# A Sinkhorn gate without GpSimd, eleven products at the attention's end, and earlier left-over tiles in the last layer

## The chip, the core and the metric

The kernel runs on one core of a Trainium2 chip. TensorE multiplies matrices into PSUM (eight banks of 128 partitions x 512 fp32 columns), VectorE (DVE), ScalarE (ACT) and GpSimd (POOL) do the element work, and SyncE (SP) issues nearly all transfers. The metric is the device time of one execution in microseconds, as the median of several runs. Lines such as L410 are lines of the kernel before.

## What is computed

Three layers follow one another. The inputs are drawn once with a fixed seed.

```python
# attention with random features: B, H, S, D = 4, 8, 576, 64; 128 features
h = proj(x) - sum(x * x) / 2;  phi = exp(h - max(h)) / sqrt(128)
out = (phi(q) @ (phi(k).T @ v)) / (phi(q) @ sum(phi(k)) + 1e-6)
# -> x of 2304 tokens x 512

# mixture of 8 experts with a balanced gate
P = np.exp(logits - logits.max())            # logits = x @ w_gate, 2304 x 8
for _ in range(8):
    P /= P.sum(1, keepdims=True) + 1e-09
    P /= P.sum(0, keepdims=True) + 1e-09
    P *= N / E
for e in range(E):
    out += P[:, e:e+1] * (np.maximum(x @ w1[e], 0.0) @ w2[e])      # 512 -> 1024 -> 512

# last layer: 512 -> 768 -> 512
h = np.maximum(np.maximum(x @ w1, x @ w2), x @ w3)
out = h @ w_out
```

## The kernel before

**Products.** Every fp32 matrix is split into a high and a low part, and the first multiplication of each layer is done by a scheme of Strassen's kind: seven products instead of eight, of sums and differences of operands. `sub_products` writes such a set. It works for half the width of the experts' middle layer at a time, so `s` counts sub-experts: s = 0 and 1 are the two halves of expert 0. One product is six matmuls of 128x384 (L410 to L412) into one of three banks, `ub`, `vb`, `wb`. Two of the three keys alternate between sets (`bu0`/`bu1`, `bv0`/`bv1`), `bw` is the same in all. ScalarE copies what is needed twice (`u1`, `u5`, `u2`, L417), VectorE adds it to a bank (`plus`, L217), and the sum is a result: (0,0) and (1,1) leave from `wb`, (0,1) from `vb`, (1,0) from `ub`. `relu_results` makes each result into a pair of high and low operands `h` (ScalarE L456, VectorE L457). A bank has 512 columns, of which a product uses Q = 384.

**Tiles.** `tile_out` is the second multiplication: six matmuls of 128x512 (L480 to L482) into one of three banks in turn (`next_r`: `r0`, `r1`, `r2`), added by VectorE to the accumulator `acc` (L495, later with the gate's weight, L502 and L503). The six tiles of one set wait in a queue, and `take()` writes one of them between two products of the next set.

**Order.** `program()` generates the products, tiles and all vector work as tasks with costs. TensorE's order is the order of the code. For the other engines and for the transfers a planner (`Tasks.ordered`) simulates the costs and chooses the order; some tasks may go to VectorE or to GpSimd. Waits between engines are derived from the tiles that instructions use, for PSUM by whole banks.

**The attention's end.** The attention runs in 16 steps of two heads, each a chain over several engines. Behind each of its last code points TensorE gets one product of the expert layer (`feed_forward()`, `next(layers)`), at most FILL = 9; then the logits of the gate (L1227, L1235), their transposes (L1245) and the rest of s = 0 and 1 follow. In these first two sets there are only three banks, so `bu0`, `bv0` and `bw` serve both.

**The gate.** `gate()` is a generator with eleven pieces; from the fourth product of s = 1 on, a piece is written before 2 of 5 products. First the maximum of all logits is found: per partition by VectorE (L655), across partitions by GpSimd (`partition_all_reduce`, L656), negated (L657), and ScalarE takes the exponential (L658). Each of eight rounds then has five VectorE operations for the rows (sum, + 1e-9, reciprocal, multiply, sums of columns: L661 to L665, with `rs` and `cs` in SBUF), a matmul with a matrix of ones that sums the columns over the partitions (L670, into one of `r0` to `r2`), and four VectorE operations (L671 to L674). The weighted tiles of the next expert need the result.

**The last layer.** It has three phases (ph 3 to 5), each of three groups n of three sets m, 7 products each; q = 7m + i counts a group's products. A group's six tiles are left over for the next group: in the first group of phase 3 one is written after each product, everywhere else after q = 3, 6, 9, ... (L951). The first sets of phases 4 and 5 read operands `x` that `load_x` brings back from memory.

Of the kernel before, what the change touches and what calls it, by code (L numbers as in the profile page):

```python
# [21 lines left out]
ORDER_1 = [(0, 0), (3, 3), (4, 4), (1, 1), (5, 5), (6, 2), (2, 6)]  # L22
ORDER_2 = [0, 2, 3, 5, 4, 1, 6]

FILL = 9
SLACK = 6000
START = [("load", 0), ("squared", 0), ("squared", 1), ("norms", 0, 0), ("v", 1), ("load", 1), ("v", 0)]

# [126 lines left out]
def tile_performer__moe__max3(ctx, tc, kq_t, kq, v1, omega2, w_gate, w1, w2, m1, m2, m3, m_out, out):  # L155
    nc = tc.nc
# [28 lines left out]
    ident = const.tile([P, P], F32, name="ident")  # L185
    prob = const.tile([P, NT, E], F32, name="prob")
    mx = const.tile([P, 2], F32, name="mx")
    rs = const.tile([P, NT, 1], F32, name="rs")
    cs = const.tile([P, 1, E], F32, name="cs")
    pt = const.tile([2 * N // 3 // P * E, P], F32, name="pt")  # L190

# [64 lines left out]
    def t_(k):  # L256
        return ts[k]
# [126 lines left out]

    u_turn = [0, 0, 1]
    r_turn = [0]

    def next_r():  # L390
# [3 lines left out]
    def sub_products(k, before, results, xs=None):  # L394


        xs = xs or x_home
        n = u_turn.pop(0)
        u_turn.append(1 - u_turn[-1])
        ub, vb, wb = f"bu{n}", f"bv{n}", "bw"  # L400

        def product(i, j, b, onto):
            before(i, j)
            kh, kl = w_keys(k, i)

            def run():
                ps, w, x = banks[b][:, :Q], ws[k][:, i].rearrange("p c (k f) -> p c k f", k=2), [xs(j, c)[0]() for c in range(2)]
                given = dict(skip_group_check=onto)
                for c in range(2):
                    nc.tensor.matmul(ps, w[:, 0, c], x[c][:, 0], start=c == 0 and not onto, stop=False, **given)  # L410
                    nc.tensor.matmul(ps, w[:, 0, c], x[c][:, 1], start=False, stop=False, **given)  # L411
# [12 lines left out]
        yield  # L424
        to_u("u1", ub)
        product(*p[1], vb, False)
        yield
        to_u("u5", vb)
        product(*p[2], ub, True)
        yield  # L430
        to_u("u2", ub)
        product(*p[3], wb, False)
        yield
        results(0, 0, wb, lambda b, plus=plus: plus(wb, wb, "u1"), ("u1", wb))
        product(*p[4], ub, True)
        yield
        results(1, 1, wb, lambda b, plus=plus: plus(wb, ub, "u5"), ("u5", ub))
        product(*p[5], vb, True)
        yield
        results(0, 1, vb, lambda b, plus=plus: plus(vb, vb, "u2"), ("u2", vb))  # L440
        product(*p[6], ub, True)
        yield
        results(1, 0, ub, None, (None, ub))
# [204 lines left out]
    def gate():  # L648
        flat = prob.rearrange("p t e -> p (t e)")

        def dve(run, r, w):
            add("D", 250, lambda e: run(), r, w)

        dve(lambda: nc.vector.memset(t_("ones"), 1.0), [], ["ones"])
        dve(lambda: nc.vector.tensor_reduce(out=mx[:, 0:1], in_=flat, axis=AX.X, op=ALU.max), ["prob", "ones"], ["mx0"])  # L655
        add("P", 3000, lambda e: nc.gpsimd.partition_all_reduce(mx[:, 1:2], mx[:, 0:1], P, bass.bass_isa.ReduceOp.max), ["mx0"], ["mx1"])  # L656
        dve(lambda: nc.vector.tensor_scalar_mul(mx[:, 1:2], mx[:, 1:2], -1.0), [], ["mx1"])  # L657
        add("A", 300, lambda e: nc.scalar.activation(flat, flat, AF.Exp, bias=mx[:, 1:2]), ["mx1"], ["prob"])  # L658
        yield
        for _ in range(8):  # L660
            dve(lambda: nc.vector.tensor_reduce(out=rs, in_=prob, axis=AX.X, op=ALU.add), ["prob"], ["rs"])  # L661
            dve(lambda: nc.vector.tensor_scalar_add(rs, rs, 1e-9), [], ["rs"])
            dve(lambda: nc.vector.reciprocal(rs, rs), [], ["rs"])
            dve(lambda: nc.vector.tensor_tensor(out=prob, in0=prob, in1=rs.to_broadcast([P, NT, E]), op=ALU.mult), ["rs"], ["prob"])
            dve(lambda: nc.vector.tensor_reduce(  # L665
                out=cs[:, 0, :], in_=prob.rearrange("p t e -> p e t"), axis=AX.X, op=ALU.add
            ), ["prob"], ["cs"])
            yield
            b = next_r()
            pe(150, lambda b=b: nc.tensor.matmul(banks[b][:, :E], t_("ones"), cs[:, 0, :], start=True, stop=True), ["ones", "cs"], [b])  # L670
            dve(lambda b=b: nc.vector.tensor_scalar_add(cs[:, 0, :], banks[b][:, :E], 1e-9), [b], ["cs"])  # L671
            dve(lambda: nc.vector.reciprocal(cs, cs), [], ["cs"])
            dve(lambda: nc.vector.tensor_scalar_mul(cs, cs, float(N) / E), [], ["cs"])
            dve(lambda: nc.vector.tensor_tensor(out=prob, in0=prob, in1=cs.to_broadcast([P, NT, E]), op=ALU.mult), ["cs"], ["prob"])  # L674
        yield
        b = next_r()
        late = prob[:, PT:, :].rearrange("p t e -> p (t e)")
        pe(110, lambda: nc.tensor.transpose(banks[b][: 2 * PT * E, :P], late, ident), ["prob"], [b])
        act(P, lambda: nc.scalar.copy(pt, banks[b][: 2 * PT * E, :P]), [b], ["pt"])
        dma(48, lambda: prob_t.rearrange("t e c -> (t e) c"), lambda: pt, ["pt"], ["prob_t"])  # L680
        yield
# [3 lines left out]
    def program():  # L685
# [19 lines left out]
        for s in range(SUBS):  # L705
            if s:
                prepare_w1(s)
            else:
                w1_store(0)
            if s == SUB_E + 1:  # L710
                for _ in gating:
                    pass
            e = s // SUB_E
            for i, _ in enumerate(sub_products(s % 2, no_loads, relu_results(s % 2))):
                if i >= (1 if s > 1 else 3):
                    take()
                if s == 1 and i == 3:
                    gating = gate()
                if gating:
                    if gate_wait[0] % 5 in (0, 2):  # L720
                        next(gating, None)
                    gate_wait[0] += 1
            while queue:
                take()
            rest = prepare_w2(s, s == 0)
            if e == 0:
                evict = evict_raw(s == 0)
            else:
# [201 lines left out]
        for ph in (3, 4, 5):  # L930
            back = ph == 4
            xs = x_beside if back else x_home
            for n in range(3):
# [3 lines left out]
                for m in range(3):  # L937
                    a = 3 * n + m
                    slot = (a + 1) % 2
                    mat = 8 - a if back else a  # L940

                    def before(i, j, a=a, slot=slot, mat=mat):
                        kh, kl = w_keys(slot, i)
                        if ph == 3 or a > 1:
                            dma(256, lambda: ws[slot][:, i].bitcast(F32), lambda: lc1[mat][i], [("lc1", mat)], kh + kl)
                        if a == 0:
                            load_x(ph, j, xs)

# [348 lines left out]
    with tc.manual_schedule():  # L1297
# [4 lines left out]
        with left as att:  # L1302
# [7 lines left out]
            ts.update({f"w2_{k}": a.tile([P, 1024], F32R, name=f"w2_{k}") for k in range(2)})  # L1310
            ts.update({f"h{k}": a.tile([P, 2, Q], F32R, name=f"h{k}") for k in range(14)})
            banks.update({k: new_bank("po") for k in ("bu0", "bv0", "bw")})
            ring["b"] = "ph"
            layers = feed_forward()
            n = 0
            for _ in steps:
                if n < FILL:
                    next(layers)
                    n += 1
        while n < FILL:  # L1320
            next(layers)
            n += 1
        banks.update({k: new_bank("ph") for k in ("bu1", "bv1", "r0", "r1")})
        banks["r2"] = new_bank("small")
        b = ctx.enter_context(tc.tile_pool(name="b", bufs=1, side="left", reuse_waits="tile"))
        ts.update({f"w2_{k}": b.tile([P, 1024], F32R, name=f"w2_{k}") for k in range(2, 7)})
        ts.update({k: b.tile([P, Q], F32, name=k) for k in ("b11", "b12", "b21", "b22", "t1", "t2", "t3", "t4")})
# [61 lines left out]
```

## Time and profile before

| | |
|---|---|
| median of three runs | 1910.83 us (1908.7 to 1912.18) |
| the profiled execution | 1908.9 us; its span 1907.1 us |
| TensorE (PE) busy | 1864.3 us, 98% of the span |
| share of the last chain on PE | 89% |
| VectorE / ScalarE / GpSimd busy | 76% / 48% / 55% |
| mean granted clock | 0.993 |

A busy share is an average over stages. Rows of the timeline have the start in us, the duration in us, engine, line, operation, output and inputs, and in brackets the idle time of the engine before it with what released it. Matmuls overlap, so the pitch from start to start counts, not the duration: 0.175 us for a 128x384 and 0.23 us for a 128x512 at the full clock.

### The profile page before, as it was taken

The page shows a single profiled execution, that of the slowest core. Times are in us where ns is not written, and L with a number is a line of the kernel's source. Part 1 is how long each engine was busy: PE and PEld are TensorE (multiplying, and loading weights), DVE is VectorE, ACT ScalarE, POOL GpSimd, SP SyncE. Part 2 cuts the span into 40 slices and gives each one's busy share as a digit, 9 for nine tenths or more (in the row PEclk, how much of TensorE's full clock was granted, in tenths as well). Part 3 has the DMA queues.
Part 4 walks back from the last instruction along what each step waited for, and adds up shares of the span by engine and source line. Part 5 has one row for each costly group of instructions (what it writes and reads, how often), then busy time and mean ns, then how long its engine had stood idle before and what let it go on. Part 6 is the DMA issues. An engine that isn't in the chain of part 4 may idle for free.

```text
span 1907.1 us, 34485 instructions
## 1 busy us (share of the span) xinstructions
PE 1864.3 (98%) x11521; PEld 1769.9 (93%) x11521; DVE 1456.7 (76%) x2639; ACT 915.9 (48%) x2180; POOL 1045.2 (55%) x970
## 2 busy tenths in 40 slices
PE   8996899999999999999999999999999999999998
PEld 6885799999999999999999999999999999989998
DVE  7875998888888767888888888988888776443445
ACT  7874355555544465454454445544544543232221
POOL 4533777676545247576766786767776754320000
PEclk9998999999999999999999999999999999999999
DMA  7655699988877999998999899999999999997573
GB/s 238 198 178 198 229 313 324 330 298 319 270 248 248 316 307 337 327 286 286 332 306 305 269 347 300 309 304 286 302 321 312 323 352 355 342 336 252 209 242 117
DMA packets 376033, 547.06 MB, mean 287 GB/s; under 512 B 31568, under 2 KB 226992, under 8 KB 375856
## 3 DMA queue, kind: packets, MB, share of 16 engines
q1 hardware_dynamic: 375856, 544.86, 84.8%
q8 instruction: 91, 1.49, 0.3%
q14 instruction: 86, 0.70, 0.1%
HBM read 392.65 MB, written 152.09 MB: 286 GB/s over the span
## 4 chain that ended last, share of the span: by engine, by line
PE 89%; DVE 4%; DMA 4%; issue 1%; ACT 1%; POOL 1%; SPq 0%; DVEq 0%; ACTq 0%; POOLq 0%
PE po L410 9%; PE po L411 8%; PE po L412 8%; PE ph L410 6%; PE ph L412 6%; PE ph L411 6%; PE ph L822 5%; PE ph L820 5%; PE ph L821 5%; PE ph L480 4%; PE ph L482 4%; PE ph L481 4%; PE small L822 3%; PE small L820 3%; PE small L821 3%; PE small L482 2%
## 5 line engine op out<-in xcount | busy, mean ns | idle before, releaser
L217 POOL TENSOR_TENSOR h<-b,h 128x384 fp32r<-128x384 f32 x149 | 163.6, 1106 | 125.5 <-ACT h L760 124.4
L410 PE MATMUL po<-x,wa 128*128 128x384 f32 x676 | 227.4, 336 | 5.1 <-DVE po L217 2.3
L411 PE MATMUL po<-x,wa 128*128 128x384 f32 x676 | 226.9, 336 | 0.0
L412 PE MATMUL po<-x,wa 128*128 128x384 f32 x676 | 226.8, 336 | 0.0
L217 POOL TENSOR_TENSOR g<-g,g 128x256 f32<-128x256 f32 (+2 forms) x164 | 163.1, 996 | 86.2 <-DVE g L217 32.4
L412 PE MATMUL ph<-x,wa 128*128 128x384 f32 x588 | 198.6, 338 | 9.3 <-DVE wa L217 9.3
L822 PE MATMUL ph<-h,w 128*128 128x384 f32 x598 | 202.3, 338 | 0.0
L820 PE MATMUL ph<-h,w 128*128 128x384 f32 x598 | 202.0, 338 | 0.0
L821 PE MATMUL ph<-h,w 128*128 128x384 f32 x598 | 201.4, 337 | 0.0
L217 DVE TENSOR_TENSOR po<-po,u 128x384 f32<-128x384 f32 x230 | 129.2, 562 | 94.2 <-PE po L412 89.9
L410 PE MATMUL ph<-x,wa 128*128 128x384 f32 x588 | 198.7, 338 | 2.4 <-DVE po L217 1.8
L411 PE MATMUL ph<-x,wa 128*128 128x384 f32 x588 | 198.1, 337 | 0.0
L217 POOL TENSOR_TENSOR h<-t,h 128x384 fp32r<-128x384 f32 x131 | 141.7, 1086 | 92.0 <-ACT h L760 76.8
L217 DVE TENSOR_TENSOR acc<-ph,acc 128x384 f32<-128x384 f32 x280 | 154.0, 551 | 48.3 <-PE ph L822 47.0
L417 ACT COPY u<-po 128x384 f32<-128x384 f32 x186 | 89.2, 481 | 158.8 <-PE po L412 154.9
L217 POOL TENSOR_TENSOR wb<-g,wb 128x512 fp32r<-128x512 f32 (+2 forms) x108 | 132.4, 1232 | 52.2 <-ACT wb L214 45.6
L760 ACT CAST h<-b 128x384 fp32r<-128x384 f32 x192 | 98.4, 515 | 123.0 <-DVE b L775 101.8
L760 ACT CAST h<-t 128x384 fp32r<-128x384 f32 x256 | 129.9, 514 | 34.2 <-POOL t L217 16.3
L417 ACT COPY u<-ph 128x384 f32<-128x384 f32 x183 | 87.8, 480 | 121.4 <-PE ph L412 120.1
L410 PEld LDWEIGHTS po<-x,wa 128*128 128x128 f32 x676 | 127.0, 188 | 7.9 <-DVE po L217 2.6
L217 POOL TENSOR_TENSOR t<-b,b 128x384 f32<-128x384 f32 x106 | 112.0, 1073 | 32.4 <-DVE b L775 29.6
L480 PE MATMUL ph<-w,h 128*128 128x512 f32 x328 | 129.7, 395 | 0.0
(223 smaller groups left out, 5444.5 us busy)
## 6 DMA issues: line engine op xcount, KB each, us to landing
wa<-wc SPq DMA_DIRECT2D x252, 256.0 KB, 5.1
w<-wc SPq DMA_DIRECT2D x124, 512.0 KB, 5.7
g<-in_moe_w_dram SPq DMA_DIRECT2D x82, 512.0 KB, 6.1
wc<-w SPq DMA_DIRECT2D x64, 512.0 KB, 6.9
g<-in_moe_w_dram SPq DMA_DIRECT2D x249, 128.0 KB, 4.7
x<-xc SPq DMA_DIRECT2D x64, 384.0 KB, 7.2
wa<-wl SPq DMA_DIRECT2D x189, 128.0 KB, 5.0
w<-wl SPq DMA_DIRECT2D x93, 256.0 KB, 5.1
```

The costliest lines, as they stand in the source:

```text
L217: (nc.gpsimd if on == "P" else nc.vector).tensor_tensor(out=out, in0=in0, in1=in1, op=op)
L410: nc.tensor.matmul(ps, w[:, 0, c], x[c][:, 0], start=c == 0 and not onto, stop=False, **given)
L411: nc.tensor.matmul(ps, w[:, 0, c], x[c][:, 1], start=False, stop=False, **given)
L412: nc.tensor.matmul(ps, w[:, 1, c], x[c][:, 0], start=False, stop=c == 1, **given)
L417: act(Q, lambda: nc.scalar.copy(t_(n), banks[b][:, :Q]), [b], [n])
L480: nc.tensor.matmul(ps, h[:, 0, c], t_(wh)[:, part], start=f == 0, stop=False)
L481: nc.tensor.matmul(ps, h[:, 0, c], t_(wl)[:, part], start=False, stop=False)
L482: nc.tensor.matmul(ps, h[:, 1, c], t_(wh)[:, part], start=False, stop=f == 1)
L760: act(Q, lambda: nc.scalar.copy(t_(h)[:, 0], t_(n)), [n], [(h, 0)])
L820: nc.tensor.matmul(ps, wv[:, 0, sub, d], h[:, 0], start=o == 0, stop=False)
L821: nc.tensor.matmul(ps, wv[:, 0, sub, d], h[:, 1], start=False, stop=False)
L822: nc.tensor.matmul(ps, wv[:, 1, sub, d], h[:, 0], start=False, stop=o == 1)
```

## The change

First, the gate: the maximum across partitions is found by a TensorE transpose, a VectorE reduction and a small matmul with ones that spreads it. Row sums and column sums lie in PSUM, in the columns 384 and up of bank `bw`, which the products leave free. A round has one VectorE operation less. The pieces are thirteen and are written before every second product. Second, the banks: `r2` is opened before the attention's end, and the first set puts its result (1,1) there; the second set uses the three banks in other roles. Eleven products stand in the attention's end, the last two behind its last two code points. Third, the last layer: in the first group of phases 4 and 5 the left-over tiles are written after each product from q = 1 on.

```diff
-FILL = 9
+FILL = 11
+FILL_AFTER = (1, 2, 3, 4, 5, 6, 7, 8, 9, 12, 14)
...
+    bank_turn = [("bw", "bv0", "bu0", "r2"), ("bu0", "bv0", "bw", "bw")]
...
-        ub, vb, wb = f"bu{n}", f"bv{n}", "bw"
+        if bank_turn:
+            ub, vb, wb, w2b = bank_turn.pop(0)
+        else:
+            n = u_turn[0]
+            u_turn[0] = 1 - n
+            ub, vb, wb, w2b = f"bu{n}", f"bv{n}", "bw", "bw"
...
-        results(1, 1, wb, lambda b, plus=plus: plus(wb, ub, "u5"), ("u5", ub))
+        results(1, 1, w2b, lambda b, plus=plus: plus(w2b, ub, "u5"), ("u5", ub))
...
+        def spare(a, b):
+            return banks["bw"][:, Q + a : Q + b]
...
-        add("P", 3000, lambda e: nc.gpsimd.partition_all_reduce(mx[:, 1:2], mx[:, 0:1], P, bass.bass_isa.ReduceOp.max), ["mx0"], ["mx1"])
-        dve(lambda: nc.vector.tensor_scalar_mul(mx[:, 1:2], mx[:, 1:2], -1.0), [], ["mx1"])
+        yield
+        pe(110, lambda: nc.tensor.transpose(spare(0, P)[0:1], mx[:, 0:1], ident), ["mx0"], ["spare"])
+        dve(lambda: nc.vector.tensor_reduce(out=mx[0:1, 1:2], in_=spare(0, P)[0:1], axis=AX.X, op=ALU.max), ["spare"], ["mx1"])
+        yield
+        pe(110, lambda: nc.tensor.matmul(spare(0, 1), t_("ones")[0:1, :], mx[0:1, 1:2], start=True, stop=True), ["ones", "mx1"], ["spare"])
+        dve(lambda: nc.vector.tensor_scalar_mul(mx[:, 1:2], spare(0, 1), -1.0), ["spare"], ["mx1"])
...
+        rs = lambda: spare(16, 16 + NT)
...
-            b = next_r()
-            pe(150, lambda b=b: nc.tensor.matmul(banks[b][:, :E], t_("ones"), cs[:, 0, :], start=True, stop=True), ["ones", "cs"], [b])
-            dve(lambda b=b: nc.vector.tensor_scalar_add(cs[:, 0, :], banks[b][:, :E], 1e-9), [b], ["cs"])
-            dve(lambda: nc.vector.reciprocal(cs, cs), [], ["cs"])
-            dve(lambda: nc.vector.tensor_scalar_mul(cs, cs, float(N) / E), [], ["cs"])
+            pe(150, lambda: nc.tensor.matmul(spare(0, E), t_("ones"), cs[:, 0, :], start=True, stop=True), ["ones", "cs"], ["spare"])
+            dve(lambda: nc.vector.tensor_scalar(spare(0, E), spare(0, E), 1e-9, E / float(N), op0=ALU.add, op1=ALU.mult), [], ["spare"])
+            dve(lambda: nc.vector.reciprocal(spare(0, E), spare(0, E)), [], ["spare"])
...
-                    if gate_wait[0] % 5 in (0, 2):
+                    if gate_wait[0] % 2 == 0:
...
-                        if len(queue) > 6 or ph == 3 and n == 0 or q >= 3 and q % 3 == 0:
+                        if len(queue) > 6 or n == 0 and (ph == 3 or q) or q >= 3 and q % 3 == 0:
...
             banks.update({k: new_bank("po") for k in ("bu0", "bv0", "bw")})
+            banks["r2"] = new_bank("small")
...
-            for _ in steps:
-                if n < FILL:
+            for n, _ in enumerate(steps):
+                if n + 1 in FILL_AFTER:
                     next(layers)
```

How the instructions stand shows where the pieces went. At the attention's end, TensorE before, from the last attention step's matmuls (`kvs`, `qpT`) to the first tile; `xs` is the attention's output being transposed, `lt` the logits, and each product stands with one of its six matmuls:

```order
L1145 MATMUL ph<-kvs,qpT 64x65 x2
L410 MATMUL po<-x_72,wb 128x384
...
L410 MATMUL po<-x_75,wb 128x384
...
L1169 MATMUL ph<-ident,xs 128x64
L1166 MATMUL ph<-ident,xs 128x128 x4
L1227 MATMUL ph<-xf_222,gate_w 32x128 x16
L1235 MATMUL ph<-xf_222,gate_w 32x128 x4
L1245 MATMUL ph<-ident,lt 128x128 x2
L410 MATMUL po<-x_76,wb 128x384
...
L480 MATMUL ph<-w_0_2583,h_2592 128x512
```

The same stretch of TensorE now:

```order
L1159 MATMUL ph<-kvs,qpT 64x65 x2
L414 MATMUL po<-x_71,wb 128x384
...
L414 MATMUL po<-x_74,wb 128x384
...
L1180 MATMUL ph<-ident,xs 128x128 x4
L414 MATMUL po<-x_75,wb 128x384
...
L1249 MATMUL ph<-xf_221,gate_w 32x128 x4
L414 MATMUL po<-x_72,wb 128x384
...
L1259 MATMUL ph<-ident,lt 128x128 x2
L484 MATMUL ph<-w_0_2582,h_2591 128x512
```

The tenth and eleventh products moved ahead of the logits and of their transposes, and the first tile follows the transposes directly.

On VectorE in the same place, before, from the divisions of the last attention step (`rc`, `xs`) to the splits of results into `h`:

```order
L1156 RECIPROCAL rc<-rc 64x2
L1158 TENSOR_TENSOR xs<-ph,rc 128x4x64 x2
L1158 TENSOR_TENSOR xs<-ph,rc 64x128
L457 SCALAR_TENSOR_TENSOR h_2594<-po,h_2594 128x384
L457 SCALAR_TENSOR_TENSOR h_2592<-po,h_2592 128x384
```

And now:

```order
L1172 TENSOR_TENSOR xs<-ph,rc 128x4x64 x2
L1172 TENSOR_TENSOR xs<-ph,rc 64x128
L217 TENSOR_TENSOR wb<-g_82,wb 128x2x256
L217 TENSOR_TENSOR po<-po,u_2581 128x384
L461 SCALAR_TENSOR_TENSOR h_2590<-po,h_2590 128x384
L461 SCALAR_TENSOR_TENSOR h_2593<-small,h_2593 128x384
```

The split of the first result (`h_2590`), which releases the eighth product's bank, stands behind the divisions now, with a weight's low half and an add ahead of it.

In the last layer, TensorE at the start of phase 4's first group, before (`x_73` and `x_77` are reloaded operands, the rows with `small` and `ph<-w` left-over tiles):

```order
L410 MATMUL po<-h_2589,wb 128x384
...
L410 MATMUL po<-x_73,wb 128x384
...
L480 MATMUL small<-w_0_2583,h_2592 128x512
...
L410 MATMUL po<-x_77,wb 128x384
...
L410 MATMUL po<-x_74,wb 128x384
```

And now:

```order
L414 MATMUL po<-h_2588,wb 128x384
...
L484 MATMUL ph<-w_0_2582,h_2591 128x512
...
L414 MATMUL po<-x_72,wb 128x384
...
L484 MATMUL small<-w_0_2582,h_2591 128x512
...
L414 MATMUL po<-x_76,wb 128x384
...
L484 MATMUL ph<-w_0_2582,h_2590 128x512
```

A tile stands between every two products there, and none is left for the group's third set.

## Rows read from the trace of the kernel before

**Rows 1.** Windows: length, busy time (instructions) of each engine, clock, DMA share, GB/s.
```profile
160.00:186.20 26.20, 16.91 (x77) 15.12 (x77) 15.22 (x32) 12.22 (x26) 7.62 (x8) 0.81 0.64 213
186.20:240.00 53.80, 48.16 (x228) 41.41 (x227) 47.78 (x103) 20.07 (x43) 43.22 (x45) 0.94 0.71 240
```

**Rows 2.** Timeline, TensorE, the attention's end.
```profile
139.96 0.41 PE L410 MATMUL po<-x,wa 128*128 128x384 f32 x1 [0.47 <-ACT u L417]
...
146.61 0.44 PE L410 MATMUL po<-x,wa 128*128 128x384 f32 x1 [2.33 <-DVE po L217]
...
151.94 0.57 PE L410 MATMUL po<-x,wb 128*128 128x384 f32 x1 [2.70 <-DVE h L457]
152.30 0.53 PE L411 MATMUL po<-x,wb 128*128 128x384 f32 x1
...
158.45 0.44 PE L1245 MATMUL ph<-ident,lt 128*128 128x128 f32 x2 [0.49 <-ACT lt L214]
159.35 0.45 PE L410 MATMUL po<-x,wb 128*128 128x384 f32 x1 [0.46 <-ACT u L417]
```

**Rows 3.** Timeline, VectorE, the same place: the splits behind the divisions.
```profile
150.41 1.47 DVE L457 SCALAR_TENSOR_TENSOR h<-po,h 128x384 fp32r<-128x384 f32 x3
```

**Rows 4.** Timeline, GpSimd, the gate's all-reduce and what follows.
```profile
167.80 0.38 POOL L656 PARTITION_ALL_REDUCE mx<-mx  x1 [5.82 <-issue]
175.72 2.48 POOL L217 TENSOR_TENSOR w<-g,w 128x512 fp32r<-128x512 f32 x2 [7.54 <-issue]
```

**Rows 5.** Timeline, VectorE (two rows), then ScalarE, up to s = 2.
```profile
178.23 0.93 DVE L217 TENSOR_TENSOR g<-g 128x256 f32<-128x256 f32 x1 [7.13 <-POOL w L217]
...
182.02 0.68 DVE L217 TENSOR_TENSOR wa<-g,wa 128x512 fp32r<-128x512 f32 x1
...
182.13 0.62 ACT L214 CAST wa<-g 128x512 fp32r<-128x512 f32 x1 [9.65 <-DVE g L217]
```

**Rows 6.** Timeline, TensorE, the second product of s = 2.
```profile
182.76 0.69 PE L412 MATMUL ph<-x,wa 128*128 128x384 f32 x1 [9.29 <-DVE wa L217]
183.24 0.52 PE L410 MATMUL ph<-x,wa 128*128 128x384 f32 x1
```

**Rows 7.** The page's transfers: operation, count, size, median us to landing.
```profile
g<-in_moe_w_dram SPq DMA_DIRECT2D x82, 512.0 KB, 6.1
```

**Rows 8.** Timeline, TensorE, matmuls of the gate.
```profile
208.42 0.60 PE L670 MATMUL small<-cs,ones 128*128 128x8 f32 x2 [3.65 <-DVE cs L665]
...
213.50 0.37 PE L410 MATMUL po<-x,wb 128*128 128x384 f32 x1
...
237.21 0.39 PE L670 MATMUL ph<-cs,ones 128*128 128x8 f32 x2 [1.00 <-DVE cs L665]
```

**Rows 9.** VectorE by line: busy us, mean ns; then one line's min/median/max ns.
```profile
L664 DVE TENSOR_TENSOR prob<-prob,rs 128x144 f32<-128x144 f32 x8 | 4.9, 614 | 0.2
...
L662 DVE TENSOR_SCALAR rs<-rs 128x18 f32<-128x18 f32 x8 | 4.8, 598 | 0.3
L674 DVE TENSOR_TENSOR prob<-prob,cs 128x144 f32<-128x144 f32 x8 | 4.5, 569 | 0.2
...
L673 DVE TENSOR_SCALAR cs<-cs 128x8 f32<-128x8 f32 x8 | 3.4, 422 | 0.3
...
L662 DVE TENSOR_SCALAR rs<-rs x8: 176/545/1219, 169.5 to 235.6; 128x18 f32<-128x18 f32 x8
...
L664 DVE TENSOR_TENSOR prob<-prob,rs x8: 295/492/1049, 170.3 to 236.2; 128x144 f32<-128x144 f32 x8
...
L671 DVE TENSOR_SCALAR cs<-ph x5: 152/157/167, 203.2 to 239.9; 128x8 f32<-128x8 f32 x5
...
L217 DVE TENSOR_TENSOR po<-po,u x11: 544/555/567, 162.8 to 255.8; 128x384 f32<-128x384 f32 x11
```

**Rows 10.** Timeline, TensorE, the last layer.
```profile
1643.96 0.45 PE L410 MATMUL ph<-x,wb 128*128 128x384 f32 x1 [1.00 <-DVE po L217]
...
1714.99 0.45 PE L410 MATMUL po<-x,wb 128*128 128x384 f32 x1 [2.36 <-DMA x<-xc]
```

More of the change, by code (lines that the diff above doesn't have):

```diff
@@ L187, in tile_performer__moe__max3 @@
     mx = const.tile([P, 2], F32, name="mx")
-    rs = const.tile([P, NT, 1], F32, name="rs")
     cs = const.tile([P, 1, E], F32, name="cs")
@@ L383, in prepare_w2 @@
         rest()
-    u_turn = [0, 0, 1]
+    bank_turn = [("bw", "bv0", "bu0", "r2"), ("bu0", "bv0", "bw", "bw")]
+    u_turn = [1]
     r_turn = [0]
@@ L397, in sub_products @@
         xs = xs or x_home
-        n = u_turn.pop(0)
-        u_turn.append(1 - u_turn[-1])
-        ub, vb, wb = f"bu{n}", f"bv{n}", "bw"
+        if bank_turn:
[4 more added lines that the diff above has]
+            ub, vb, wb, w2b = f"bu{n}", f"bv{n}", "bw", "bw"
         def product(i, j, b, onto):
@@ L655, in gate @@
         dve(lambda: nc.vector.tensor_reduce(out=mx[:, 0:1], in_=flat, axis=AX.X, op=ALU.max), ["prob", "ones"], ["mx0"])
-        add("P", 3000, lambda e: nc.gpsimd.partition_all_reduce(mx[:, 1:2], mx[:, 0:1], P, bass.bass_isa.ReduceOp.max), ["mx0"], ["mx1"])
-        dve(lambda: nc.vector.tensor_scalar_mul(mx[:, 1:2], mx[:, 1:2], -1.0), [], ["mx1"])
+        yield
[4 more added lines that the diff above has]
+        dve(lambda: nc.vector.tensor_scalar_mul(mx[:, 1:2], spare(0, 1), -1.0), ["spare"], ["mx1"])
         add("A", 300, lambda e: nc.scalar.activation(flat, flat, AF.Exp, bias=mx[:, 1:2]), ["mx1"], ["prob"])
         yield
+        rs = lambda: spare(16, 16 + NT)
         for _ in range(8):
[L661 to L664, printed above, removed]
+            dve(lambda: nc.vector.tensor_reduce(out=rs(), in_=prob, axis=AX.X, op=ALU.add), ["prob"], ["rs"])
+            dve(lambda: nc.vector.tensor_scalar_add(rs(), rs(), 1e-9), [], ["rs"])
+            dve(lambda: nc.vector.reciprocal(rs(), rs()), [], ["rs"])
+            dve(lambda: nc.vector.tensor_tensor(
+                out=prob, in0=prob, in1=rs().unsqueeze(2).to_broadcast([P, NT, E]), op=ALU.mult
+            ), ["rs"], ["prob"])
             dve(lambda: nc.vector.tensor_reduce(
@@ L668, in gate @@
             yield
-            b = next_r()
-            pe(150, lambda b=b: nc.tensor.matmul(banks[b][:, :E], t_("ones"), cs[:, 0, :], start=True, stop=True), ["ones", "cs"], [b])
-            dve(lambda b=b: nc.vector.tensor_scalar_add(cs[:, 0, :], banks[b][:, :E], 1e-9), [b], ["cs"])
-            dve(lambda: nc.vector.reciprocal(cs, cs), [], ["cs"])
-            dve(lambda: nc.vector.tensor_scalar_mul(cs, cs, float(N) / E), [], ["cs"])
-            dve(lambda: nc.vector.tensor_tensor(out=prob, in0=prob, in1=cs.to_broadcast([P, NT, E]), op=ALU.mult), ["cs"], ["prob"])
+            pe(150, lambda: nc.tensor.matmul(spare(0, E), t_("ones"), cs[:, 0, :], start=True, stop=True), ["ones", "cs"], ["spare"])
+            dve(lambda: nc.vector.tensor_scalar(spare(0, E), spare(0, E), 1e-9, E / float(N), op0=ALU.add, op1=ALU.mult), [], ["spare"])
+            dve(lambda: nc.vector.reciprocal(spare(0, E), spare(0, E)), [], ["spare"])
+            dve(lambda: nc.vector.tensor_tensor(
+                out=prob, in0=prob, in1=spare(0, E).unsqueeze(1).to_broadcast([P, NT, E]), op=ALU.mult
+            ), ["spare"], ["prob"])
         yield
@@ L1312, in tile_performer__moe__max3 @@
             banks.update({k: new_bank("po") for k in ("bu0", "bv0", "bw")})
+            banks["r2"] = new_bank("small")
             ring["b"] = "ph"
             layers = feed_forward()
-            n = 0
-            for _ in steps:
-                if n < FILL:
+            for n, _ in enumerate(steps):
+                if n + 1 in FILL_AFTER:
                     next(layers)
[L1319 to L1322, printed above, removed]
         banks.update({k: new_bank("ph") for k in ("bu1", "bv1", "r0", "r1")})
-        banks["r2"] = new_bank("small")
         b = ctx.enter_context(tc.tile_pool(name="b", bufs=1, side="left", reuse_waits="tile"))
```

## The prediction

> **What bounds the kernel now.** I read the share of busy time first: TensorE is busy for 1864.3 of the 1907.1 us span, and the chain that ended last runs through it for 89%. Its matmuls are not touched in number or size, apart from two tiny ones more, so the only time to be had is where TensorE stands idle or runs at its lower clock. The 20-us windows put nearly all of that at three places: the end of the attention, the 80 us behind it, and a spot near 1715 us. So I went through TensorE's timeline there, and then through the engine named as releaser at each gap. The stage behind the attention, cut at its longest gap, reads: 16.91 us busy in 26.20 at a granted clock of 0.81, then 48.16 in 53.80 at 0.94 [rows 1]. What the reader is to see: TensorE waits there for vector engines, not for its own work.
>
> **The attention's end: four banks, eleven products.** Gaps of 0.47, 2.33, 2.70, 0.49 and 0.46 us end at 139.96, 146.61, 151.94, 158.45 and 159.35 [rows 2]. After the 2.70 the next matmul starts 0.36 us later [rows 2], and the twelve of two products go at a pitch of 0.32 instead of the usual 0.175 us: the lower level, 1.2 GHz, 1.7 us more.
> The 2.33 waits for VectorE's adds on a bank that the seventh product reuses. With the fourth bank that add has its own place, and in the order the seventh product waits only for an early one: 2.33 goes. The 0.47 is of the same kind (a ScalarE copy out of a bank) and I count half of it.
> The 2.70 stays. The eighth product reuses the bank of result (0,0), and VectorE splits that result only behind the divisions of the last attention step. Before, three splits (1.47 us, [rows 3]) stood between the divisions and the release; now it is a weight's low half, an add and one split, about 0.6 + 0.5 + 0.55 = 1.65. So the wait moves up with everything, grows by 0.2, and I leave it its 1.7 us of low clock. The tenth and eleventh products now lie in the 0.49 and 0.46, which copies of the logits and of a bank cause; each product is 1.05 us of independent work, so both go. Sum: 2.33 + 0.25 - 0.2 + 0.95 = 3.3, taken as **-3.5** (between 2.5 and, if the clock doesn't fall, 5.2).
>
> **GpSimd out of the gate.** GpSimd's all-reduce ran 0.38 us, but GpSimd stands 5.82 us ahead of it and 7.54 us behind it with nothing that it waits for [rows 4]: from 161.98, where its work before ends, to 175.72 it does nothing else. Queued behind it is the weight arithmetic of the next sub-expert (s=2). VectorE waits 7.13 us for it, to 178.23, ScalarE 9.65, to 182.13 [rows 5], and TensorE 9.29, to 182.76; then eleven matmuls go at the 0.32 pitch [rows 6], 11 x 0.145 = 1.6 us. The replacement costs a transpose, a reduction of 1 x 128, a one-column matmul and a multiply: of TensorE about 0.5 us (the nearest row is the gate's matmul pair, 0.39 at 237.21 [rows 8]); the VectorE pair under 0.5.
> The Trainium skill (GPSIMD Engine Reference, on loading code) says that the first call of a freshly loaded library routine pays about 6 us; the 5.82 agrees, and what the 7.54 behind it is that page does not say.
> What is late next? The raw weights of s=2. Such a load takes 6.1 us to land [rows 7], and behind the landing stands a chain of casts and differences, about 4.5 us on VectorE (178.23 to 182.70, [rows 5]). Both fit before TensorE asks, but barely: I walk the new order with traced durations and get a wait of 1.1 us at the second product of s=2, and no fall of the clock (after the gap of 1.00 it did not fall, [rows 8]). 9.29 + 1.6 - 1.1 - 0.2 = **-9.6** (from -5, load late by 5, to -11).
>
> **The rounds of the gate.** From 186.2 to 240 us TensorE is idle for 53.80 - 48.16 = 5.64 us [rows 1], the longest waits 3.65 at 208.42 and 1.00 at 237.21; behind the 3.65 the gate's matmul pair and twelve more take until 213.50, 5.08 us where 2.7 is usual: 2.4 of low clock [rows 8]. Together 8.0. The releaser is VectorE, which is busy for 47.78 of the 53.80 us [rows 1]. Why are its rounds so long? Four operations on SBUF operands vary wildly: the add to the row sums 0.18 to 1.22 us, the multiply 0.30 to 1.05; means 0.60, 0.61, 0.57 and 0.42 [rows 9]. The one that reads PSUM stays at 0.15 to 0.17, and the far bigger add of PSUM and SBUF at 0.54 to 0.57 [rows 9]. GpSimd works beside it for most of the stage. The change puts both sums into PSUM, so all the varying operations get a PSUM operand or, the fourth (0.42), go. Per round that is (0.60 - 0.18) + (0.61 - 0.30) + (0.57 - 0.30) + 0.42 = 1.4 us; over the 7.5 rounds of this stretch 10.6. No row shows an operation in place in PSUM; the bounds are the 0.16 of the one that reads it (nearest, taken) and the means as traced.
> VectorE's load becomes 47.8 - 10.6 = 37.2 us in a stretch of 53.8 - 8.0 = 45.8: 81% instead of 89, without the long lumps. Against it: the rounds come every 2 products instead of 2.5, and the spare columns lie in the bank of the products' third accumulator. The order follows waits by whole banks, so the row sums wait for the result's add to leave, the next product into that bank for the gate's multiply, and the small matmul for both. I walk three rounds with the shortest durations and find waits of 0.25, 0.7 and 0.15; over the stage I leave 2.2 us. **-5.8** (from 0 to -8).
> By the Trainium skill (VectorE: DVE Perf Modes, the table of its errata section) an operation with a PSUM source costs 120 cycles plus its length where one from SBUF costs 58, 65 ns more at 0.96 GHz; an estimate by that page makes seven operations a round, eight rounds, 3.6 us of VectorE dearer. The row speaks against it, 0.157 for 128 x 8 from PSUM beside 0.176 at best for 128 x 18 from SBUF [rows 9].
>
> **The last layer.** At 1714.99 TensorE waits 2.36 us for a reloaded operand, and runs at the low clock until 1718.8 [rows 10]: twelve matmuls, 1.7 us more by the pitch above, and another 0.3 of smaller waits. In the new order four tiles of 1.38 us stand ahead of that product instead of one, 4.1 us of work that does not need the operand; the loads are issued as before. So -4.4 (the bound is 0, if the loads are delayed by as much). The price: the first group of the first phase already shows what its third sub-product does without tiles between the products: 1.00 us [rows 10], and with a slow first matmul 1.16. Now the first group of both later phases has that form: 2 x 1.16. **-2.1** (from +2.3 to -4.4).
>
> **Sum.** The profiled execution took 1908.9 us. 1908.9 - 3.5 - 9.6 - 5.8 - 2.1 = 1887.9. The median of the runs shown is 1.9 above that execution, so 1889.8; I say **1889**.
>
> **The rivals.**
> *VectorE becomes the bound in the gate.* If operations with one SBUF operand still vary, VectorE loses only the fourth, 7.5 x 0.42 = 3.2: 44.6 us of work for 45.8, at 2 products a round more than TensorE's pace. The stage then gives nothing back: 1908.9 - 15.2 + 1.9 = 1896. For it: GpSimd now has 13.7 us of postponed work in the same stretch. Against it: the two rows in PSUM never vary.
> *Weights late.* The 55 us of transfer time between 160 and 240 us (0.64 x 26.2 + 0.71 x 53.8, [rows 1]) have to go through in 62; where the raw load lands 5 us late, and the clock falls again (1.6), 1889 + 6 = 1895. Against it: over the whole kernel such loads land in 6.1 us [rows 7].
> *One bank, two users: slower.* TensorE's product into the shared bank waits for the gate, the gate's next matmul waits for the product's result to be evicted, and each round costs a full wait. Priced by the one round that shows it, 3.65 + 2.4 = 6.0, eight rounds are 48 against the 8 that go: 1908.9 - 15.2 + 40 + 1.9 = 1936. It makes the kernel slower from 2.9 us a round on (23.2 us of gains over eight rounds). Against it: between two uses of that bank lie other products and tiles, some 4.8 us. The Trainium skill (PSUM — Partial Sum Buffer, on bank collisions) says that two engines may not touch one bank in the same partitions at once, even in other columns, and wants waits by bank; the order's waits are so, and no row here shows their price.
> *The change doesn't do what it says.* GpSimd's 7.54 has no cause in the trace. If s=2 is late for another reason that is hidden now, the gap shrinks to that of 208.42, 3.65 with 2.4 of clock: 9.3 + 1.6 - 6.0 = 4.9 of the 9.6 remain, 1894, and with the last layer at nothing 1896.
>
> **How the numbers follow.** The forecast has 0.60, VectorE as bound 0.15, weights late 0.10, not as said 0.10, the shared bank 0.05, of which 0.04 ends above the old time. Two tenths may be left out: the slow case, and the far ends of the sums. Low: every term at its better end, 5.2 + 11 + 8 + 4.4 = 28.6, gives 1882; I take 1881. High: the three rivals on the fast side end at 1896, with a clock fall more 1898; I take 1899. About 0.2%, 3.8 us, is what a measurement of this kernel can tell from no change. Faster by more 0.94, within 0.02, slower 0.04.
>
> **What would show it.** GpSimd's idle 13.7 us gone, and no gap over 2 us before s=2; the row-sum add at 0.2 us in all rounds; no wait of 3 us at a gate matmul; the eighth product still waiting for a split, 2 to 3 us; no wait for a reload near 1700 us, and two new waits of 1 us in the last phases' third sub-products. Wrong would be: a granted clock below 0.95 anywhere from 160 to 240, or small waits at every product into the shared bank that sum to over 5 us.

## The result

The changed kernel takes 1888.07 us at the median (1886.86 to 1889.63, four runs) against 1909.76 of the kernel before, a ratio of 0.9888 with a 95% interval of 0.987 to 0.9905. It is 21.7 us faster; forecast were 1889 and 21.0 in the sum of the steps. The profiled execution took 1889.63 us, its span is 1887.9; the profiled execution of the kernel before took 1908.9, so the two traces read here lie 19.3 us apart.

The page's head shows TensorE's own work unchanged (1862.0 beside 1864.3 us busy) in a shorter span, and the last chain runs on it for 94% where it was 89:

```profile
span 1887.9 us, 34457 instructions
...
PE 1862.0 (99%) x11524; PEld 1767.7 (94%) x11524; DVE 1460.3 (77%) x2637; ACT 918.1 (49%) x2180; POOL 1038.3 (55%) x964
...
PE 94%; DVE 3%; DMA 2%; ACT 1%; issue 0%; SPq 0%; POOL 0%; DVEq 0%; ACTq 0%
```

The windows of the stage behind the attention, cut at the first tile of s = 2 (the columns are those of [rows 1]), have the granted clock at 1.00 where it was 0.81 and 0.94, and TensorE idle for 0.97 us of the second stretch where it was 5.64 [rows 1]:

```profile
160.00:173.66 13.66, 12.26 (x58) 9.88 (x58) 12.22 (x23) 9.67 (x21) 6.60 (x8) 1.00 0.99 332
173.66:220.00 46.34, 45.37 (x228) 39.70 (x228) 40.20 (x107) 22.42 (x47) 40.59 (x41) 1.00 0.81 285
```

TensorE's timeline has these waits left, to be held against [rows 2, 6, 8, 10]: the eighth product, the transpose of the maximum, one gate matmul, and the third sets of the first groups of phases 4 and 5.

```profile
149.46 0.69 PE L414 MATMUL po<-x,wb 128*128 128x384 f32 x1 [3.63 <-DVE h L461]
149.95 0.52 PE L415 MATMUL po<-x,wb 128*128 128x384 f32 x1
...
165.20 0.27 PE L664 MATMUL po<-ident,mx 128*1 128x128 f32 x1 [1.23 <-DVE h L461]
...
217.08 0.39 PE L683 MATMUL po<-cs,ones 128*128 128x8 f32 x2 [0.96 <-DVE po L217]
...
1719.38 0.45 PE L414 MATMUL po<-x,wb 128*128 128x384 f32 x1 [1.02 <-DVE po L217]
...
1812.09 0.44 PE L414 MATMUL ph<-x,wb 128*128 128x384 f32 x1 [0.98 <-DVE po L217]
```

GpSimd's two long stands of [rows 4] are gone. Between the first tile and that of s = 2 its longest idle times are these, each with an engine that it waits for:

```profile
164.15 1.80 POOL L217 TENSOR_TENSOR g<-g 128x256 f32<-128x256 f32 x2 [3.21 <-DVE w L217]
...
173.58 2.55 POOL L217 TENSOR_TENSOR w<-g,w 128x512 fp32r<-128x512 f32 x2 [3.40 <-ACT w L214]
```

VectorE's operations of a round no longer vary (name, count, min/median/max in ns; compare the single lines of [rows 9]):

```profile
L674 DVE TENSOR_SCALAR po<-po x8: 183/184/184, 174.2 to 213.5; 128x18 f32<-128x18 f32 x8
...
L676 DVE TENSOR_TENSOR prob<-prob,po x8: 294/304/305, 174.7 to 214.0; 128x144 f32<-128x144 f32 x8
...
L686 DVE TENSOR_TENSOR prob<-prob,po x8: 303/304/305, 183.8 to 218.5; 128x144 f32<-128x144 f32 x8
```

Where the time came from is read by taking the start of the same instruction in both traces. The last column is what the step added to the lead. One s is a quarter of an expert's middle layer (256 of its 1024 columns, not half of it): s = 0 to 3 are expert 0, and the first weighted tiles are those of s = 4, the first set of expert 1.

| place | before, us | after, us | lead | of this step |
|---|---|---|---|---|
| a product in the attention's end, ahead of all changes | 139.96 | 139.15 | 0.8 | 0.8 |
| first tile | 161.57 | 157.45 | 4.1 | 3.3 |
| first tile of s = 2 | 186.12 | 173.66 | 12.5 | 8.3 |
| seventeenth tile from there, in s = 4 | 238.59 | 218.48 | 20.1 | 7.7 |
| a weighted tile near the middle layer | 664.05 | 644.18 | 19.9 | -0.2 |
| near the end of phase 3 (VectorE) | 1692.02 | 1674.94 | 17.1 | -2.8 |
| in phase 4 | 1757.56 | 1737.13 | 20.4 | 3.4 |
| near the end of phase 5 | 1883.27 | 1864.09 | 19.2 | -1.3 |

The four steps of the change sum to 3.3 + 8.3 + 7.7 + 2.1 = 21.4 us. The 2.8 us lost in between belong to no step: between the same two places the ten profiled kernels told of below need 1025.4 to 1031.5 us (before 1028.0, after 1030.8) with the same code there, so one profiled execution of each tells nothing about that stretch. Stages are therefore compared by leads inside them. That their 21.4 is close to the 21.7 of the medians is in part chance: the two traces themselves end 19.2 us apart.

### The profile page after: what moved, and what is told of

The parts are those of the page before. It is cut to its first block, busy times and chain, and to the rows that moved or that the text cites. A ratio compares the mean times of both kernels' runs of the same rounds, so it can differ in the third digit from the quotient of the medians.

```text
span 1887.9 us, 34457 instructions
## 1 busy us (share of the span) xinstructions
PE 1862.0 (99%) x11524; PEld 1767.7 (94%) x11524; DVE 1460.3 (77%) x2637; ACT 918.1 (49%) x2180; POOL 1038.3 (55%) x964
## 4 chain that ended last, share of the span: by engine, by line
PE 94%; DVE 3%; DMA 2%; ACT 1%; issue 0%; SPq 0%; POOL 0%; DVEq 0%; ACTq 0%
PE po L414 9%; PE po L415 9%; PE po L416 9%; PE ph L414 7%; PE ph L416 6%; PE ph L415 6%; PE ph L835 5%; PE ph L836 5%; PE ph L834 5%; PE ph L486 4%; PE ph L484 4%; PE ph L485 4%; PE small L835 3%; PE small L836 3%; PE small L834 3%; PE small L484 2%
## 5 line engine op out<-in xcount | busy, mean ns | idle before, releaser
L217 POOL TENSOR_TENSOR g<-g,g 128x256 f32<-128x256 f32 (+2 forms) x158 | 158.1, 1002 | 95.1 <-DVE g L217 42.7
L484 PE MATMUL ph<-w,h 128*128 128x512 f32 x328 | 129.4, 395 | 0.7 <-ACT h L465 0.7
L486 PE MATMUL ph<-w,h 128*128 128x512 f32 x328 | 129.1, 394 | 0.3 <-DVE h L466 0.3
```

What stands on the lines that cost most here:

```text
L217: (nc.gpsimd if on == "P" else nc.vector).tensor_tensor(out=out, in0=in0, in1=in1, op=op)
L484: nc.tensor.matmul(ps, h[:, 0, c], t_(wh)[:, part], start=f == 0, stop=False)
L486: nc.tensor.matmul(ps, h[:, 1, c], t_(wh)[:, part], start=False, stop=f == 1)
```

## Experiments

Times are medians, with the median of the kernel before from the same session in brackets, and the 95% interval of the ratio to it. The kernel before moves by up to 1.6 us from session to session, so a difference between two medians is good to some 2 us; the traces settle smaller ones.

**The gate of before in the changed kernel.** GpSimd's all-reduce, sums in SBUF, the old pace:

```diff
...
+        add("P", 3000, lambda e: nc.gpsimd.partition_all_reduce(mx[:, 1:2], mx[:, 0:1], P, bass.bass_isa.ReduceOp.max), ["mx0"], ["mx1"])
...
+            dve(lambda: nc.vector.tensor_scalar_add(rs, rs, 1e-9), [], ["rs"])
...
-                    if gate_wait[0] % 2 == 0:
+                    if gate_wait[0] % 5 in (0, 2):
```

> The changed kernel with the gate of before: GpSimd's all-reduce, sums in SBUF, a piece before 2 of 5 products. Theory: the gate was worth two terms, GpSimd's absence (8 to 10 us at s = 2) and the VectorE waits of the rounds (6 to 8), so this kernel takes 1888 + 16 = 1904, from 1902 to 1906, and the trace shows again a GpSimd idle of some 7 us behind the all-reduce, and waits of 1 to 4 us at gate matmuls. Rival (the eleven products or the bank roles took the gap at s = 2 away): under 1897.

Measured: 1904.3 (1908.25), 0.9968 to 0.9987. GpSimd's and TensorE's timelines have the old pattern back:

```profile
165.28 0.38 POOL L661 PARTITION_ALL_REDUCE mx<-mx  x1 [5.92 <-issue]
174.42 3.70 POOL L218 TENSOR_TENSOR w<-g,w 128x512 fp32r<-128x512 f32 x3 [8.76 <-issue]
...
180.86 0.69 PE L417 MATMUL ph<-x,wa 128*128 128x384 f32 x1 [11.13 <-DVE wa L218]
...
206.34 0.39 PE L675 MATMUL small<-cs,ones 128*128 128x8 f32 x2 [3.11 <-DVE cs L670]
```

So the gate is worth 16 us by the medians and 16.1 by the lead at the first weighted tile, and neither banks nor products took the wait at s = 2 away: with the earlier attention's end it even grows from 9.29 to 11.13.

**All-reduce beside the new gate.** To take GpSimd's absence alone:

```diff
...
+        add("P", 3000, lambda e: nc.gpsimd.partition_all_reduce(mx2[:, 0:1], mx[:, 0:1], P, bass.bass_isa.ReduceOp.max), ["mx0"], ["mx2"])
```

> The changed kernel, and beside it GpSimd does the old all-reduce of the same values into a tile that nobody reads. Theory: GpSimd's absence alone makes s = 2 late, whoever needs the maximum: a wait of 6 to 9 us before s = 2 and a low clock after it, 1895 to 1899, the GpSimd idle of over 12 us in all is there again. Rival (the wait was the chain maximum to exponential to rows on VectorE and ScalarE): within 2 us of 1888, though GpSimd stands as long.

Measured: 1892.21 (1908.25), 0.9903 to 0.9933. The forecast time was missed by 3 us, but the trace has the mechanism. GpSimd, VectorE, and TensorE, one after the other:

```profile
173.00 0.49 POOL L664 PARTITION_ALL_REDUCE mx<-mx  x1 [7.12 <-PE po L669]
180.88 1.01 POOL L218 TENSOR_TENSOR h<-b,h 128x384 fp32r<-128x384 f32 x1 [7.39 <-issue]
...
185.10 0.42 DVE L218 TENSOR_TENSOR g<-g,g 128x256 f32<-128x256 f32 x1 [7.70 <-POOL g L218]
...
190.21 0.59 PE L685 MATMUL po<-cs,ones 128*128 128x8 f32 x2 [7.24 <-ACT h L461]
```

Nobody reads the result, and yet VectorE stands for 7.70 us behind GpSimd's next weight operation and TensorE for 7.24. It falls not on s = 2 but on a gate matmul, since the all-reduce runs 15.6 us after the first tile here (6.2 in the kernel before), with the weights of s = 2 done. Where the first weighted tile is added, this trace is 8.2 us behind that of the changed kernel; at the end 3.7, and the medians lie 4.1 apart. Of what came back, 2.9 us did so evenly from 229 to 644 us, where TensorE waits in neither trace for 0.4 us or more and its matmuls merely follow one another 0.7% faster here, at a granted clock of 1.00 in both; why is open, and the rest lies in the stretch with its spread of some 6 us.

The wait is caused by GpSimd standing, not by the chain through the maximum; that much is shown. The trace of the kernel before agrees: there the maximum was negated and the rows and column sums of the first round were done by 171.09, over 11 us before TensorE's wait ended at 182.76.

```profile
168.21 0.15 DVE L657 TENSOR_SCALAR mx<-mx 128x1 f32<-128x1 f32 x1 [2.47 <-POOL mx L656]
...
170.67 0.42 DVE L665 TENSOR_REDUCE cs<-prob 128x8 f32<-128x144 f32 x1
```

Why GpSimd stands so long behind the all-reduce no run shows.

**Sums in SBUF again.** All else of the new gate stays:

```diff
-        rs = lambda: spare(16, 16 + NT)
+        rs = lambda: rst
...
-            dve(lambda: nc.vector.tensor_scalar(spare(0, E), spare(0, E), 1e-9, E / float(N), op0=ALU.add, op1=ALU.mult), [], ["spare"])
-            dve(lambda: nc.vector.reciprocal(spare(0, E), spare(0, E)), [], ["spare"])
+            dve(lambda: nc.vector.tensor_scalar(cs[:, 0, :], spare(0, E), 1e-9, E / float(N), op0=ALU.add, op1=ALU.mult), ["spare"], ["cs"])
+            dve(lambda: nc.vector.reciprocal(cs, cs), [], ["cs"])
...
```

> The changed kernel with the two sums in SBUF again; the transpose, the matmuls into the spare columns, the pace and one operation less a round stay. Theory: the add to the row sums and the two multiplies vary again (means near 0.6 instead of 0.18 and 0.30, about 1 us a round), VectorE is later by 8 us of work and TensorE waits at gate matmuls: 1888 + 2 to 6 = 1890 to 1894. Rival (the missing fourth operation and the pace did it): within 1 us of 1888, with short waits only.

Measured: 1894.4 (1908.53), 0.9908 to 0.9938, 6 us slower than the changed kernel. VectorE by line in the gate's stretch (busy us, mean ns), and two of five waits at gate matmuls:

```profile
L687 DVE TENSOR_TENSOR prob<-prob,cs 128x144 f32<-128x144 f32 x8 | 6.5, 814 | 0.3
...
L677 DVE TENSOR_TENSOR prob<-prob,rst 128x144 f32<-128x144 f32 x8 | 5.5, 686 | 0.2
...
L675 DVE TENSOR_SCALAR rst<-rst 128x18 f32<-128x18 f32 x8 | 4.0, 506 | 0.3
...
183.72 0.39 PE L684 MATMUL po<-cs,ones 128*128 128x8 f32 x2 [1.60 <-DVE po L218]
...
223.11 0.39 PE L684 MATMUL po<-cs,ones 128*128 128x8 f32 x2 [2.33 <-DVE po L218]
```

The three operations take 0.81, 0.69 and 0.51 where they take 0.30, 0.30 and 0.18 in PSUM: 1.2 us a round, 9.7 in eight. The trace is 7.6 us behind at the first weighted tile. Where the sums lie is what the rounds gained by.

What the lengths in SBUF go with can be read in the trace of the kernel before. Two adds to the row sums (L662) there, the slow one beside a GpSimd operation, the fast one while GpSimd was idle from 210.15 to 215.82:

```profile
197.40 1.30 POOL L217 TENSOR_TENSOR wb<-g,wb 128x512 fp32r<-128x512 f32 x1 [1.03 <-ACT wb L214]
197.52 1.22 DVE L662 TENSOR_SCALAR rs<-rs 128x18 f32<-128x18 f32 x1
...
209.14 1.01 POOL L217 TENSOR_TENSOR b<-b,t 128x384 f32<-128x384 f32 x1
210.89 0.18 DVE L662 TENSOR_SCALAR rs<-rs 128x18 f32<-128x18 f32 x1
215.82 0.74 POOL L217 TENSOR_TENSOR g<-g,g 128x256 f32<-128x256 f32 x1 [5.67 <-DVE g L217]
```

Of the 32 executions of L662, L664, L673 and L674, nine overlap no GpSimd operation, and they take 0.17 to 0.18 (adds, small multiplies) and 0.29 to 0.31 us (multiplies by rows or columns); the others take up to 1.34. In the changed kernel all 24 of the operations above run beside a GpSimd operation, and none is slowed. No run took GpSimd's work away by itself.

**The pace of before with the new gate.**

```diff
-                    if gate_wait[0] % 2 == 0:
+                    if gate_wait[0] % 5 in (0, 2):
```

> The changed kernel with a piece of the gate before 2 of 5 products instead of every second: the thirteen pieces then take 32 products instead of 26. Theory: the pace is not what gained; VectorE has more room, the wait of 1 us at a gate matmul goes, and the time is the same or up to 1 us less, 1887 to 1888.5. Rival (the later end of the gate holds up the first weighted tiles): 1889 to 1891.

Measured: 1895.05 (1908.53), 0.9913 to 0.9943, 7 us slower. Both sides of the expectation were wrong. The gate is finished before s = 5 whatever the pace (L710); from the fourth product of s = 1 that is 4 + 21 = 25 products, which hold 13 pieces at one in two, but 10 at two in five. The last three pieces were written with nothing between them; from here until the low clock that follows is over, the trace's lag behind that of the changed kernel grows from 3.5 to 9.6 us:

```profile
229.10 0.39 PE L683 MATMUL po<-cs,ones 128*128 128x8 f32 x2 [2.52 <-DVE cs L679]
...
230.37 0.38 PE L692 MATMUL ph<-ident,prob 128*96 128x128 f32 x1 [0.88 <-DVE prob L686]
```

So the pace of one in two is what thirteen pieces need; whether it is a gain in itself this run does not show. What a slower pace with a later end would do was not tried.

**Another bank for the sums.**

```diff
-            return banks["bw"][:, Q + a : Q + b]
+            return banks["bv1"][:, Q + a : Q + b]
```

> The changed kernel with the gate's sums in the spare columns of another bank, bv1, which the products use only in every second set from s = 2 on. Theory: the wait of 1.2 us at the transpose of the maximum (165.2 us, for a split out of bank bw) goes, later waits at gate matmuls stay under 1 us: 1886.5 to 1888. Rival (the shared bank costs nothing, VectorE's place in the order does): within 0.5 us of 1888, the wait of 1.2 only moves.

Measured: 1889.03 (1908.53), 0.9878 to 0.9911. In `bv1` the gate's matmuls can stand between two products that are summed there, and this kernel seems to leave part of those sums out, which is argued and not shown; only its time is read. That lies 1.0 and 0.5 us outside the two expectations, less than two medians can tell apart. By the Trainium skill (PSUM — Partial Sum Buffer, on the matmul accumulator) a second group started in a bank makes the open one overwrite where it should add; no run here takes that apart. The wait at the transpose went, and another stood in its place:

```profile
172.63 0.42 PE L414 MATMUL ph<-x,wa 128*128 128x384 f32 x1 [1.64 <-DVE mx L668]
```

**Only the maximum in other banks.** The transpose and the spreading use the tiles' banks in turn:

```diff
-        pe(110, lambda: nc.tensor.transpose(spare(0, P)[0:1], mx[:, 0:1], ident), ["mx0"], ["spare"])
+        b = next_r()
+        pe(110, lambda b=b: nc.tensor.transpose(banks[b][0:1, :P], mx[:, 0:1], ident), ["mx0"], [b])
...
```

> The changed kernel with only the transpose and the spreading of the maximum in banks of the tiles (r0 to r2 in turn) instead of the spare columns of bw; the sums of the rounds stay in bw. Theory: the wait of 1.2 us at the transpose is a wait for another user of bank bw (a split out of it, in other columns), so it goes: 1887 us. Rival (as the run with the sums in bv1 hints): the wait only moves to the next place, the weights of s = 2, and the time stays within 0.5 us of 1888.

Measured: 1888.36 (1908.21), 0.9877 to 0.991, the rival's number, though the medians alone cannot tell it from 1887. In the trace the wait moved to the low half of the weights of s = 2:

```profile
171.83 0.45 PE L416 MATMUL ph<-x,wa 128*128 128x384 f32 x1 [0.73 <-DVE wa L217]
```

From the first tile to that of s = 2 are 16.06 us, and 16.21 in the changed kernel. The shared bank delays the transpose, but the weights are the later limit.

**The attention's end of before**, three banks and nine products:

```diff
-FILL_AFTER = (1, 2, 3, 4, 5, 6, 7, 8, 9, 12, 14)
+FILL = 9
...
-            ub, vb, wb, w2b = bank_turn.pop(0)
+        n = u_turn.pop(0)
+        u_turn.append(1 - u_turn[-1])
+        ub, vb, wb, w2b = f"bu{n}", f"bv{n}", "bw", "bw"
...
-            banks["r2"] = new_bank("small")
...
+        banks["r2"] = new_bank("small")
```

> The changed kernel with the banks and the nine products of before. Theory: the attention's end gives back 3.5 to 4.1 us and nothing else moves: 1891.5 to 1892.5. The trace shows the wait of 2.3 us at the seventh product again, and the two of 0.5 at the logits. Rival: the later start is taken up by the wait for the weights of s = 2, and it stays within 1 us of 1888.

Measured: 1893.88 (1908.25), 0.9911 to 0.994: 5.8 us by the medians, more than expected. The trace has the old waits of 2.33, 2.70, 0.49 and 0.46 to the hundredth and is 3.2 us behind at the first tile. At the first tile of s = 2 it is only 1.8 behind: TensorE comes later, the transpose of the maximum does not wait, and the stretch takes 14.85 us where the changed kernel needs 16.21. So the rival was right for 1.4 us of the gain. The 4.2 us by which it is behind at the end say nothing of this stage: near 1120 us the trace had caught up (0.1 us ahead), and it fell back at one wait in code that is the same, 5.38 us where the changed kernel's trace has 1.80:

```profile
160.64 0.39 PE L479 MATMUL ph<-w,h 128*128 128x512 f32 x1
...
175.49 0.39 PE L479 MATMUL ph<-w,h 128*128 128x512 f32 x1
...
1134.28 0.69 PE L409 MATMUL ph<-x,wa 128*128 128x384 f32 x1 [5.38 <-DVE po L216]
```

What the attention's end is worth in the whole time lies between 1.8 us by the trace and 5.8 by the medians; no run narrows it.

**The last layer's tiles of before.**

```diff
-                        if len(queue) > 6 or n == 0 and (ph == 3 or q) or q >= 3 and q % 3 == 0:
+                        if len(queue) > 6 or ph == 3 and n == 0 or q >= 3 and q % 3 == 0:
```

> The changed kernel with the left-over tiles of the last layer as before. Theory: the wait for the reloaded operand comes back with its low clock (3.3 us by the leads of the two traces) and the third set's wait goes in two phases (1.2 each): 1890.2, from 1889.5 to 1891. Rival: operands arrive in time anyway since the whole kernel runs 17 us earlier, and it is 2.4 faster: 1885.7.

Measured: 1888.84 (1908.25), 0.9884 to 0.9914. The wait for the operand is there again, though all runs 17 us earlier:

```profile
1697.53 0.69 PE L414 MATMUL po<-x,wb 128*128 128x384 f32 x1 [2.38 <-DMA x<-xc]
```

By the traces phase 4 loses 2.6 us and phase 5 wins 1.5: 1.2 in all, half of what was expected. The two products from the wait on take 3.64 us here and 4.00 in the kernel before, phase 5 wins 0.2 more, and some 0.3 us lie in waits too short to name.

**Both ends of the last layer.** Phase 4 writes four tiles ahead of the operand and keeps two for the third set; phase 5 is as before:

```diff
-                        if len(queue) > 6 or n == 0 and (ph == 3 or q) or q >= 3 and q % 3 == 0:
+                        if len(queue) > 6 or ph == 3 and n == 0 or ph == 4 and n == 0 and q in (1, 2, 3, 4) or q >= 3 and q % 3 == 0 and not (ph == 4 and n == 0 and q < 15):
```

> The changed kernel with phase 4's first group writing its tiles after q = 1, 2, 3, 4, 15 and 18, and phase 5's as before. Theory: the four tiles ahead of the reloaded operand are all that is needed, and the third set's wait of 1.2 us goes in both phases: 1888.1 - 2.3 = 1885.8. Rival: the products behind the fourth tile, now without tiles, wait for the next reload or for their banks: 1887 to 1889.

Measured: 1885.52 (1908.53), 0.9861 to 0.989. No wait of half a microsecond is left in phases 4 and 5 until the last tiles; the lead over the changed kernel grows there by 1.9 us, which speaks for the theory (2.3). Together with the maximum in other banks:

> The maximum in the tiles' banks and phase 4's tiles after q = 1, 2, 3, 4, 15 and 18, phase 5's as before the change. Theory: the two gains add, 1.2 and 2.3: 1884.5. Rival (the wait at the transpose only moves): as the run with the tiles alone, 1885.5.

Measured: 1885.17 (1908.21), 0.9863 to 0.9901. The medians cannot tell the two expectations apart; the traces can: from the first tile to that of s = 2 are 16.02 us here and 16.22 in the run with the tiles alone. The second gain is 0.2 us and not 1.2.

## Why the prediction was right, point by point

**The attention's end, 3.5 forecast, 3.3 measured.** The wait at the seventh product and the two at the logits went. The eighth product's wait grew to 3.63 where I had 2.9 (and 2 to 3 as a sign): the weight's low half ahead of the split took 1.47 us, not 0.6.

```profile
147.01 1.47 DVE L217 TENSOR_TENSOR wb<-g,wb 128x512 fp32r<-128x512 f32 x1
```

GpSimd works on SBUF beside it, from 146.66 to 147.92. By the leads, the seventh product gave 2.57 us (2.33 in the forecast), the eighth took 0.92 (0.2), the low clock behind it, nine matmuls instead of twelve, gave 0.2 (nothing), and the logits gave 1.43 (0.95), since the work around those two waits is covered too. So errors of both signs cancel; that the sum of 3.3 was taken as 3.5 rests on no row. The 0.25 for the wait at 139.96 was wrong: it stands there unchanged, 0.48. And 3.3 is the best case: from that product to the first tile the changed kernel's trace takes 18.30 us, the nine other traces with this attention's end 18.39 to 19.66, longer mostly where the low clock lasts longer, and the two with the old one take 21.61 and 21.48. The gain at the first tile is thus 1.8 to 3.3.

**GpSimd, 9.6 forecast, 8.3 measured.** The gap and its low clock went whole: between the two first tiles 24.55 us became 16.21, and eleven of these 24.55 were the gap and the clock. Mis-sized was what is late next. I had 1.1 us at the weights of s = 2 and 0.2 for the new matmuls; the transpose waits 1.23 for a split out of the shared bank, the small matmul and the weights take the rest of 2.6. The run with the maximum elsewhere shows that the weights would have taken nearly all of it. The run with the old attention's end shows where the 1.3 lies: there the same stretch takes 14.85 us, 9.7 less than in the kernel before, so the first step gives some 1.4 back here. That it does so by coming 3.2 us earlier to weights that are not ready, and not by the banks' new roles, is likely from the two runs together, but no run separates it. Transfers were close to the rival: their share is 0.99 up to the first tile of s = 2 (0.93 in an equally long stretch from 160 us of the kernel before, whose 0.64 holds the gap too), and VectorE waits 0.56 for the load itself:

```profile
168.18 1.12 DVE L217 TENSOR_TENSOR g<-g 128x256 f32<-128x256 f32 x1 [0.56 <-DMA g<-in_moe_w_dram]
```

**The rounds, 5.8 forecast, 7.7 measured.** The reason held and the size of the rest was too large: VectorE is busy for 40.20 of 46.34 us, 87% where I had 81, and yet TensorE has one wait of 0.96 where I left 2.2 in small ones. That the steadier lengths count for more than the load is argued from this, not shown. That the sums in SBUF cost 6 us at the median and 7.6 in the trace shows that the first rival, at 7, was priced about right and hangs on the condition that it named.

**The last layer, 2.1 forecast, 2.1 measured**, 3.4 won in phase 4 and 1.3 lost in phase 5. The traces of the run with the old tiles give only 1.2 and its medians 0.8, so its size lies between 1 and 2 us.

**The slower rival** (a shared bank in each of eight rounds) did not occur: one wait of 1.23, one of 0.96. The median of the forecast, 1889, was within 1 us, in part by luck: the errors of the second and third step, 1.3 and 1.9, have opposite signs, and so have those within the first.

## What to carry to other kernels

An engine that does one rare operation can hold up all the work queued behind it: count its idle time on both sides of the operation, and price that by the engines that follow. Short VectorE operations on SBUF that take several times their best length beside a busy GpSimd were steadied here by giving one operand a place in PSUM, in free columns of a bank in use, at times when no sum was open in it. And a gap that goes shows the next one: here the wait at the transpose, taken away twice, came back at the next operand.

## What was not expected of the hardware

The all-reduce costs GpSimd more behind it than ahead: 5.82 and 7.54 us in the kernel before, 5.92 and 8.76 in the first experiment, and 7.39 behind it in the second. The Trainium skill (GPSIMD Engine Reference, on dispatch) states only a cost of about 6 us ahead of a first call. And in-place operations in PSUM were nearly as fast as the best in SBUF: 184 ns beside 176 for 128x18, 304 at the median beside 295 for the multiply. By the Trainium skill (VectorE: DVE Perf Modes, the table of its errata section) the estimate was 65 ns more for a source in PSUM; the larger of the two differences is 9 ns.
